# Idle products in float32, and a cast moved from GpSimd to VectorE, in the opening of a Fourier-filter and ELU-network kernel

## The chip, the core and the metric

The kernel runs on one core of a Trainium2 chip. A core has five engines that work at the same time, each through its own queue of instructions in order: TensorE (matrix products; PE in the profile, with PEld for its weight loads), VectorE (DVE), ScalarE (ACT), GpSimd (POOL) and SyncE (SP, which issues most transfers). They share an on-chip memory (SBUF) and the accumulation banks that TensorE writes (PSUM). Sixteen DMA engines move data; GpSimd's transfers appear in the profile as queue q0, SP's as q1, and instruction fetches as q8 and q14.

The metric is the device time of one execution in microseconds (us), lower is better. Three runs of the kernel before took 878.45, 878.87 and 879.24 us; their median is 878.87.

## What is computed

Eight sequences of 3008 positions and 256 channels go through a Fourier filter and then, as 24064 tokens, through a two-layer network with ELU between the layers:

```python
X = np.fft.rfft(x, axis=1)                  # x: (8, 3008, 256)
Yr = Xr @ w_r - Xi @ w_i + b_r              # complex product with a 256 x 256 weight
Yi = Xr @ w_i + Xi @ w_r + b_i
Yr, Yi = soft_threshold(Yr, 0.01), soft_threshold(Yi, 0.01)
y = np.fft.irfft(Yr + 1j * Yi, n=3008, axis=1)
h = y.reshape(24064, 256) @ w_in            # 256 x 2048
g = np.where(h > 0, h, np.exp(np.minimum(h, 0)) - 1)
out = g @ w_out                             # 2048 x 256
```

## The kernel before

**Tiling.** 3008 is 47 x 64, and each transform is two stages of small matrix products with a re-arrangement through DMA between them. For every sequence ("batch" below) there are the units

- A: the first stage of the forward transform, six units. `unit_A` multiplies a part of x (tiles `xt0` to `xt2`) by the matrix `M1` and copies the PSUM result to a tile `A`; in the opening a transfer (`place`, L194, on SP's queue) then puts it into the tile `Z`, which holds the arrangement that the next stage needs;
- X: the second stage, eight units. `unit_X` multiplies `Z` by `M2` into the tile `XT` (8 products of 96 columns a unit, L234);
- M: the product with the complex weight, from `wcat_r` = [w_r | w_i] and `wcat_s` = [-w_i | w_r], with bias and soft threshold, giving tiles `Y`;
- B and Y: the two stages of the inverse transform (`Bz`, stored to the DRAM tile `DB`, loaded again as `Bs`, and then `yT`, the tokens).

The network runs over 376 steps (`front`, `elu`, `back`), each of which takes 512 tokens and two of the 16 blocks of hidden units. TensorE multiplies by w_in (L1071), ScalarE takes the exponential (L1083), GpSimd and VectorE finish ELU (L1122, L1112), TensorE multiplies by w_out (L1143). The transform of the next batch is spread over the steps of the present one.

**The opening.** Batch 0 has nothing to hide behind, so its transform stands alone ahead of the first step. Its order is written out by hand (`manual_schedule`): each engine executes the instructions in the order in which the source issues them.

1. Constants. GpSimd makes index rows, issues the six loads of batch 0's x, and later waits for w_r and w_i (`w_r_f`, `w_i_f`, two loads on SP's queue). VectorE computes the angles of M1, M2 and M3; ScalarE takes the sines.
2. The six A units (`fA`). ScalarE copies each result, SP issues the placement into Z: nine transfers for the six units. Behind these on SP's queue stand the loads of w_r and w_i, three small ones of the bias, and the first quarter of w_in (`load_w_in(0)`).
3. The eight X units. Their PSUM banks are three tiles of two banks (`pre2`), and unit 7 takes two single banks (`apart`). X0, X2, X4, X6 and half of X7 are copied by ScalarE; X1, X3, X5 and the other half of X7 by VectorE.
4. The M units and the inverse of batch 0, with VectorE's scaling of w_in's quarters (`scale_w_in`, L919) put between.

**Idle products.** TensorE's granted clock depends on how busy it has been, and the kernel multiplies a tile of ones (`busy`, 128 x 512 in bfloat16) by itself into a PSUM bank that nobody reads. `idle_pe(n)` issues n such products (L601): 12 ahead of the A units, 0, 0, 1, 2, 2, 0 after the six A units (in `fA`, L831), 21 between the A and the X units (L890), and one after each of X0, X1 and X2 (L940). The 21 use a second bank, which a copy of the last A unit has to release.

**GpSimd between w_i and batch 1.** Four casts to bfloat16 make wcat_r and wcat_s (L871 to L874); the last, L874, is the negated one. Then come the identity `idm` (L875), three loads of batch 1's x of 1 MB each (`load_x`, L118) and half of w_out, also 1 MB (`load_w_out`, L914), all on queue q0.

**After the X units.** VectorE takes the absolute value of M3's angles (L952), the bias copy (L961), two multiplications for M3 (L962, L965), then threshold steps (L346, L399), bias additions (L292) and the scalings of w_in. `load_w_in(1)` is issued in the M stage, behind a store of DB on SP's queue.

The lines in question, as they stand:

```python
        pool.tensor_copy(wcat_r[:, :, D : 2 * D], w_i_f[:])
        pool.tensor_scalar(wcat_s[:, :, 0:D], w_i_f[:], -1.0, None, ALU.mult)
        pool.tensor_scalar(idm[:], prow, pcol[:], None, ALU.is_equal)
    ...
    load_w_in(0)
    for ci in range(3):
        load_x(1, ci)
    load_w_out(0)
    for u in range(8):
        unit_X(0, u, alone=True, on_dve=u in (1, 3, 5), apart=u == 7)
        if u < 3:
            idle_pe(1)
```

Of the kernel before, what the change touches and what calls it, by code (L numbers as in the profile page):

```python
# [8 lines left out]
ALU = mybir.AluOpType  # L9
AF = mybir.ActivationFunctionType  # L10
BF16 = mybir.dt.bfloat16
F32 = mybir.dt.float32
# [17 lines left out]
def kernel(  # L30
# [11 lines left out]
    nc = tc.nc  # L42
    P = nc.NUM_PARTITIONS

    B, S, D = x.shape
# [17 lines left out]
    wcat_s = constp.tile([P, 2, 2 * D], BF16, name="wcat_s")  # L63
# [157 lines left out]
    def unit_X(b, u, alone=False, on_dve=False, apart=False):  # L221
        g, dt = (u % 4, u // 4) if b > 1 else (u // 2, u % 2)
        if u == 0:
            XT_of[b] = xtp.tile([P, 2, 2, K1 * N2], BF16, name="XT", tag="XT")
        XT = XT_of[b]
        if apart:
            psv = [t[:].rearrange("p (k j) -> p k j", j=P) for t in two_banks(pre1, "mps1")]
        else:
            ps = unit_ps("xps", alone)
            psv = [ps[:].rearrange("p a (k j) -> p (a k) j", j=P)]  # L230
        nk = 8 // len(psv)
        for kk in range(8):
            k = 8 * g + kk
            nc.tensor.matmul(  # L234
                psv[kk // nk][:, kk % nk, 0 : 4 * K1],
                lhsT=Z[:, k, dt * P : dt * P + P],
                rhs=M2[:, k].rearrange("p c m -> p (c m)"), start=True, stop=True,
            )
        for h, v in enumerate(psv):
            k0 = 8 * g + nk * h  # L240
            evac(
                XT[:, dt].rearrange("p c (m s) -> p c m s", s=NS)[:, :, :, k0 : k0 + nk],
                v[:, :, 0 : 4 * K1].rearrange("p k (c m) -> p c m k", c=2),
                bool(h) if apart else on_dve,
            )
# [348 lines left out]
    busy = constp.tile([P, 512], BF16, name="busy")  # L594
    nc.vector.memset(busy[:], 1.0)
    ips = [pre1.tile([P, 512], F32, name="ips", tag="mps1")]

    def idle_pe(n):

        for _ in range(n):  # L600
            nc.tensor.matmul(ips[-1][:], lhsT=busy[:, 0:P], rhs=busy[:], start=True, stop=True)  # L601

    bias_p = wk4.tile([P, 2 * D], BF16, name="bias_p", tag="Bs")
    nc.vector.memset(bias_p[:], 0.0)
    idle_pe(12)
    xts = []
    for ci in range(3):
        xt = constp.tile([P, 8, D], F32R, name=f"xt{ci}")
        xts.append(xt)
    with tc.tile_pool(name="stagep", bufs=1) as stagep:  # L610
# [24 lines left out]
        w_r_f, w_i_f = (wk3.tile([P, 2, D], F32, name="yb", tag="yb") for _ in range(2))  # L635
# [7 lines left out]
        dve, pool = nc.vector, nc.gpsimd  # L643
# [161 lines left out]
        def sines(g, c):  # L805
            nc.scalar.activation(
                M2[:, 16 * g : 16 * g + 16, c, :],
                (v2, a2)[c][g][:].rearrange("p s k t -> p s (k t)"), AF.Sin,
                bias=0.0, scale=TURN * (1.0 + c),
            )  # L810
# [17 lines left out]

        def fA(u):
            unit_A(0, u, alone=True, apart=u == 5)  # L830
            idle_pe((0, 0, 1, 2, 2, 0)[u])  # L831

        points(0)
        wraps(0)
# [12 lines left out]
        for u in range(3):  # L847
            fA(u)
        fA(3)
        fA(4)  # L850
        fA(5)
        for k in range(3):
# [18 lines left out]
        pool.tensor_copy(wcat_r[:, :, 0:D], w_r_f[:])  # L871
        pool.tensor_copy(wcat_s[:, :, D : 2 * D], w_r_f[:])
        pool.tensor_copy(wcat_r[:, :, D : 2 * D], w_i_f[:])
        pool.tensor_scalar(wcat_s[:, :, 0:D], w_i_f[:], -1.0, None, ALU.mult)  # L874
        pool.tensor_scalar(idm[:], prow, pcol[:], None, ALU.is_equal)  # L875
        for k in range(3):
            nc.sync.dma_start(bias_p[32 * k : 32 * k + 1, :], bps[:, k])
# [9 lines left out]
        dve.tensor_scalar(w3[:], v3[:], CMAGIC, -CMAGIC, ALU.add, ALU.add)  # L887
        dve.tensor_tensor(w3[:], v3[:], w3[:], ALU.subtract)  # L888
        sines(1, 1)
        idle_pe(21)  # L890

    gatep = ctx.enter_context(tc.tile_pool(name="gatep", bufs=2))
    late2 = ctx.enter_context(tc.tile_pool(name="late2", bufs=2))
# [42 lines left out]
    load_w_out(0)  # L936
    for u in range(8):
        unit_X(0, u, alone=True, on_dve=u in (1, 3, 5), apart=u == 7)
        if u < 3:
            idle_pe(1)  # L940
    zeroth.close()
    pre2, pre1 = (
        first.enter_context(
# [402 lines left out]
```

## Time and profile before

| | us |
|---|---|
| runs: median (lowest to highest) | 878.87 (878.45 to 879.24) |
| the profiled execution: its time | 877.70 |
| the profiled execution: its span | 875.9 |
| TensorE busy in the span | 864.6 |
| ScalarE busy | 712.5 |
| VectorE busy | 667.7 |
| GpSimd busy | 584.6 |

The profile is a record of one execution: for each instruction its engine, start and length, and for each transfer when its packets moved. The span goes from the first to the last instruction; the profiled execution's own time, 877.70, lies 1.8 above its span and 1.17 below the median of the runs. Rows of a timeline read "start, length, engine, source line, operation, result<-operands, shapes, count", where a bracket gives the idle time ahead of the instruction and what ended it. The starts and lengths of matrix products overlap, because they are pipelined. Rows of a stretch read "from:to, length, busy time of each engine (instructions), granted TensorE clock as a share of full speed, busy share of the DMA engines, GB/s". The lines that carry the argument stand in the prediction.

### The profile page before, as it was taken

The page shows a single profiled execution, that of the slowest core. Times are in us where ns is not written, and L with a number is a line of the kernel's source. Part 1 is how long each engine was busy: PE and PEld are TensorE (multiplying, and loading weights), DVE is VectorE, ACT ScalarE, POOL GpSimd, SP SyncE. Part 2 cuts the span into 40 slices and gives each one's busy share as a digit, 9 for nine tenths or more (in the row PEclk, how much of TensorE's full clock was granted, in tenths as well). Part 3 has the DMA queues.
Part 4 walks back from the last instruction along what each step waited for, and adds up shares of the span by engine and source line. Part 5 has one row for each costly group of instructions (what it writes and reads, how often), then busy time and mean ns, then how long its engine had stood idle before and what let it go on. Part 6 is the DMA issues. An engine that isn't in the chain of part 4 may idle for free.

```text
span 875.9 us, 18565 instructions
## 1 busy us (share of the span) xinstructions
PE 864.6 (99%) x6779; PEld 676.4 (77%) x6779; DVE 667.7 (76%) x1118; ACT 712.5 (81%) x1247; POOL 584.6 (67%) x852
## 2 busy tenths in 40 slices
PE   8999999999999999999999999999999999999997
PEld 5568677877788877887778877787877887787776
DVE  8698778687776877768867788677777777788775
ACT  6678788888978889798887988879888798876664
POOL 6662550798757886588856888459874697734664
PEclk9999999999999999999999999999999999999999
DMA  7898337643384324743365432653337313250111
GB/s 239 278 256 242 104 93 200 183 134 85 101 241 141 97 74 124 238 126 104 93 178 163 158 105 77 191 163 126 100 82 223 93 34 91 73 145 25 35 40 49
DMA packets 115852, 116.11 MB, mean 133 GB/s; under 512 B 11552, under 2 KB 106528, under 8 KB 112400
## 3 DMA queue, kind: packets, MB, share of 16 engines
q1 hardware_dynamic: 109504, 87.40, 35.3%
q0 software_dynamic: 5968, 27.26, 9.7%
q8 instruction: 53, 0.87, 0.4%
q14 instruction: 39, 0.32, 0.1%
q10 hardware_dynamic: 288, 0.26, 0.1%
HBM read 53.28 MB, written 48.23 MB: 116 GB/s over the span
## 4 chain that ended last, share of the span: by engine, by line
PE 91%; DVE 4%; POOL 3%; issue 1%; DMA 0%; ACT 0%; SPq 0%; DVEq 0%; POOLq 0%
PE ps_o L1143 39%; PE hps L1071 34%; PE mps L324 5%; PE xps L234 3%; PE mps L1071 2%; PE yps L586 2%; PE bps L425 2%; PE aps L188 2%; PE mps L282 2%; POOL Y L340 1%; POOL yb L336 0%; POOL clip L339 0%; DVE gT L1112 0%; PE pre L282 0%; POOL Y L369 0%
## 5 line engine op out<-in xcount | busy, mean ns | idle before, releaser
L1112 DVE SCALAR_TENSOR_TENSOR gT<-Et,hps 128x512 fp32r<-128x512 f32 x630 | 403.0, 683 | 136.4 <-POOL Et L1122 126.6
L1143 PE MATMUL ps_o<-w_out_r,gT 128*128 128x256 f32 x3008 | 477.4, 302 | 0.0
L1143 PEld LDWEIGHTS ps_o<-w_out_r,gT 128*128 128x128 f32 x3008 | 404.3, 189 | 48.1 <-DVE osb L1155 0.2
L1122 POOL TENSOR_SCALAR Et<-Et 128x512 f32<-128x512 f32 x482 | 287.3, 615 | 209.2 <-ACT Et L1083 207.7
L1071 PE MATMUL hps<-yT,w_in_s 128*128 128x512 bf16 (+7 forms) x1620 | 366.2, 353 | 0.2
L1083 ACT ACTIVATE Et<-hps 128x512 f32<-128x512 f32 x514 | 282.5, 610 | 41.2 <-PE hps L1071 37.4
L1071 PEld LDWEIGHTS <-w_in_s 128*128 128x128 bf16 x1728 | 144.0, 98 | 104.0 <-issue 12.0
L1081 ACT ACTIVATE Et<-hps 128x512 f32<-128x512 f32 x192 | 104.5, 597 | 42.1 <-PE hps L1071 41.7
L1086 ACT ACTIVATE Et<-Et 128x512 f32<-128x512 f32 x192 | 110.5, 632 | 0.0
L340 POOL TENSOR_TENSOR Y<-yb,clip 128x512 bf16<-128x512 f32 x72 | 92.7, 1288 | 6.0
L336 POOL TENSOR_TENSOR yb<-yb,bias_bc 128x256 f32<-128x256 f32 x72 | 53.2, 739 | 11.3 <-DVE yb L331 11.2
L147 ACT CAST XT<-xps 128x768 bf16<-128x768 f32 x58 | 46.6, 804 | 17.0 <-PE xps L234 17.0
L331 DVE TENSOR_TENSOR yb<-mps,yb 128x512 f32<-128x512 f32 x72 | 49.8, 692 | 7.2
L147 ACT CAST yT<-yps 128x752 bf16<-128x752 f32 x56 | 44.1, 787 | 13.7 <-PE yps L586 13.5
L1114 DVE SCALAR_TENSOR_TENSOR gT<-hps,Et 128x512 fp32r<-128x512 f32 x78 | 50.2, 686 | 3.6 <-PE hps L1071 0.5
L147 ACT CAST A<-aps 128x1024 bf16<-128x1024 f32 x41 | 41.7, 1019 | 10.7 <-PE aps L188 4.9
L339 POOL TENSOR_SCALAR clip<-yb 128x512 f32<-128x512 f32 x72 | 44.1, 613 | 6.3
L147 ACT CAST Bz<-bps 128x1024 bf16<-128x1024 f32 x41 | 41.6, 1014 | 5.3 <-PE bps L425 5.0
L330 DVE TENSOR_TENSOR yb<-mps,bias_bc 128x256 f32<-128x256 f32 x72 | 30.5, 423 | 17.5 <-PE mps L324 15.7
L324 PE MATMUL mps<-wcat_s,XT 128*128 128x256 bf16 x288 | 43.3, 273 | 0.0
L1155 DVE COPY osb<-ps_o 128x512 f32<-128x512 f32 x46 | 31.7, 690 | 5.4 <-PE ps_o L1143 3.4
L234 PE MATMUL xps<-M,Z 128*128 128x96 bf16 x504 | 33.1, 211 | 2.8 <-DVE A L888 2.2
(203 smaller groups left out, 671.2 us busy)
## 6 DMA issues: line engine op xcount, KB each, us to landing
xt<-in_x_dram POOLq DMA_DIRECT2D x21, 1024.0 KB, 5.4
out_dram<-osb SPq DMA_DIRECT2D x158, 128.0 KB
Bs<-DB SPq DMA_DIRECT2D x30, 384.0 KB
Yx<-Y SPq DMA_DIRECT2D x168, 64.0 KB
DA<-A SPq DMA_DIRECT2D x19, 512.0 KB
DB<-Bz SPq DMA_DIRECT2D x19, 512.0 KB
Z<-DA SPq DMA_DIRECT2D x21, 384.0 KB
xt<-in_x_dram POOLq DMA_DIRECT2D x6, 512.0 KB, 6.4
```

The source lines that it names most:

```text
L147: nc.scalar.copy(dst, src)
L234: nc.tensor.matmul(psv[kk // nk][:, kk % nk, 0 : 4 * K1], lhsT=Z[:, k, dt * P : dt * P + P], rhs=M2[:, k].rearrange("p c m -> p (c m)"), s ...
L324: nc.tensor.matmul(out_, lhsT=lhs[:, dt] if lhs is not None else sum_of(dt, ch)[:, oc : oc + P], rhs=w[:, dt, :], start=(dt == 0), stop=(d ...
L336: nc.gpsimd.tensor_tensor(yb[:, D : 2 * D], yb[:, D : 2 * D], bias_bc[:, D : 2 * D], ALU.add)
L340: nc.gpsimd.tensor_tensor(Y_of[b, q][:, i, :], yb[:], clip[:], ALU.subtract)
L1071: nc.tensor.matmul(hps[s][:, c0:c1], lhsT=w_in_s[:, dt, ft * P : ft * P + P], rhs=yT_of[b][:, dt, t0 : t0 + c1 - c0], start=(dt == 0), sto ...
L1081: nc.scalar.activation(Et[:, s], hps[s], AF.Relu, scale=-1.0)
L1083: nc.scalar.activation(Et[:, s], hps[s], AF.Exp)
L1086: nc.scalar.activation(Et[:, s], Et[:, s], AF.Exp, scale=-1.0)
L1112: nc.vector.scalar_tensor_tensor(o, e, -1.0, h, ALU.add, ALU.max)
L1122: nc.gpsimd.tensor_scalar(e, e, 1.0, 0.0, ALU.min, ALU.max)
L1143: nc.tensor.matmul(po[q][:, i_ % 2, :], lhsT=gT[:, s, i_ * P : i_ * P + P], rhs=w_out_r[:, ft, :], start=(ft == 0 and i_ % 2 == 0), stop=( ...
```

## The change

Three edits, all in the opening. An idle product now reads the same tile as float32, 128 x 256, with its 256 columns taken twice, and there are 3 and 6 of them where there were 12 and 21. Those between the A units and between the X units go. The negated cast of w_i goes from GpSimd, where it stood ahead of the identity, to VectorE, between its copies of X5 and X7.

```diff
     def idle_pe(n):
 
+        ones = busy[:].bitcast(F32)
         for _ in range(n):
-            nc.tensor.matmul(ips[-1][:], lhsT=busy[:, 0:P], rhs=busy[:], start=True, stop=True)
+            nc.tensor.matmul(
+                ips[-1][:].rearrange("p (a b) -> p a b", a=2), lhsT=ones[:, 0:P],
+                rhs=ones.unsqueeze(1).to_broadcast([P, 2, 256]), start=True, stop=True,
+            )
...
-    idle_pe(12)
+    idle_pe(3)
...
         def fA(u):
             unit_A(0, u, alone=True, apart=u == 5)
-            idle_pe((0, 0, 1, 2, 2, 0)[u])
...
-        pool.tensor_scalar(wcat_s[:, :, 0:D], w_i_f[:], -1.0, None, ALU.mult)
...
-        idle_pe(21)
+        idle_pe(6)
...
     for u in range(8):
         unit_X(0, u, alone=True, on_dve=u in (1, 3, 5), apart=u == 7)
-        if u < 3:
-            idle_pe(1)
+        if u == 5:
+            nc.vector.tensor_scalar(wcat_s[:, :, 0:D], w_i_f[:], -1.0, None, ALU.mult)
```

Source lines of the changed kernel lie 2 to 4 higher from here on: the idle products are L602, the cast L942.

## The prediction

> **What bounds the kernel now.** I read the page first, then stretches of the span, then the order of time in the first 50 us. On the page TensorE is busy 99% of the span.
>
> ```profile
> PE 864.6 (99%) x6779; PEld 676.4 (77%) x6779; DVE 667.7 (76%) x1118; ACT 712.5 (81%) x1247; POOL 584.6 (67%) x852
> ```
>
> The stretches (length, then busy us of PE, PEld, DVE, ACT, POOL, granted clock, DMA share, GB/s) show where that average hides something:
>
> ```profile
> 30.00:57.00 27.00, 25.75 (x219) 13.64 (x218) 21.82 (x40) 21.45 (x44) 14.06 (x19) 1.00 1.03 309
> 57.00:873.00 816.00, 813.26 (x6381) 645.01 (x6379) 621.75 (x1003) 671.99 (x1182) 550.37 (x780) 1.00 0.43 124
> ```
>
> From 57 us on TensorE idles 2.7 us in 816, so whatever is gained or lost before that is carried to the end one for one; no edit touches anything later. The opening is latency. Its chain of waits reads (start, length, what):
>
> ```profile
> 22.34 0.61 issue
> 22.95 0.62 PE xps L234 x8
> 23.57 0.43 PE ips L601
> 24.00 0.64 PE xps L234 x8
> ...
> 28.34 0.81 ACT XT L147
> ```
>
> Two places decide. The first is X0, the X unit that starts at 22.95. The second is VectorE, which stands still until 43.60 for a transfer (timeline of VectorE; brackets: idle before, and what ended it):
>
> ```profile
> 43.60 0.43 DVE L919 TENSOR_SCALAR w_in_s<-w_in_f 128x512 bf16<-128x512 f32 x1 [1.48 <-DMA w_in_f<-in_moe_w_in_dram]
> 43.94 0.68 DVE L346 SCALAR_TENSOR_TENSOR Y<-mps,clip 128x512 bf16<-128x512 f32 x1
> ...
> 45.34 0.74 DVE L399 SCALAR_TENSOR_TENSOR Y<-mps,gT 128x256 bf16<-128x256 f32 x2
> ```
>
> Behind that one wait stand two L346, a copy and both L399, which end at 46.08, and the inverse transforms need those. Why is this second quarter of w_in late? It travels on SP's queue (q1), issued behind a store of DB. Two DMA views, of 36 to 39 us and of 39 to 43 us (MB, share of 16 engines):
>
> ```profile
> q0 software_dynamic: 881, 1.08, 143.4%
> ```
>
> ```profile
> q1 hardware_dynamic: 1640, 1.21, 92.5%
> ```
>
> From 36 to 39 only GpSimd's queue (q0) moves data; SP's follows when that is drained. So w_in lands when it does because of when GpSimd issued batch 1's x and half of w_out:
>
> ```profile
> 25.03 1.51 POOL L874 TENSOR_SCALAR wcat_s<-yb 128x512 bf16<-128x512 f32 x1
> 26.52 0.62 POOL L875 TENSOR_SCALAR idm<-prow,pcol 128x128 bf16<-128x128 f32 x1
> 27.09 1.86 POOL L118 DMA_DIRECT2D xt<-in_x_dram  x3
> ```
>
> ```profile
> 25.50:26.00 0.50, 0.13 (x1) 0.50 0.00 0
> ```
>
> The last row (length, DVE busy, clock, DMA share, GB/s) says that the DMA engines stood empty just before.
>
> **The change part by part.**
>
> *The cast leaves GpSimd.* L874's 1.51 us go. The identity, three x loads and w_out behind it move up by that, x to 25.6, into an empty stretch of DMA. q0 drains 1.5 us sooner, and so do, on q1, the DB stores, w_in's second quarter and the Bs load that waits for the last DB store: w_in lands at 42.1. VectorE then needs the 2.48 us that it needs now (43.60 to 46.08): L399 ends at 44.6. Gain on this path 1.5.
>
> *The cast joins VectorE,* between X5's copy and X7's. Its nearest relative is the scaling of w_in:
>
> ```profile
> L919 DVE TENSOR_SCALAR w_in_s<-w_in_f x6: 419/557/809, 38.1 to 55.8; 128x512 bf16<-128x512 f32 x6
> ```
>
> I take the median, 0.56 us; 0.42 and 0.81 are the ends. Nothing hides it, since X7's products are ready by then; X7's half copy, L952 and M's second product, which needs this weight, queue behind it. The idle products removed from X pay for it:
>
> *No products between X units.* The chain shows 0.43 us for each of three, among X units of 0.64, all at half clock:
>
> ```profile
> 23.00:23.20 0.20, 0.20 (x6) 0.95 0.83 276
> ...
> 26.60:26.80 0.20, 0.20 (x9) 1.00 0.00 0
> ```
>
> ```profile
> L145 DVE CAST XT<-xps 128x768 bf16<-128x768 f32 x3 | 2.8, 955 | 3.5 <-PE xps L234 3.5
> ```
>
> ```profile
> 28.68 0.56 DVE L145 CAST XT<-mps 128x384 bf16<-128x384 f32 x1
> 29.15 1.08 DVE L952 TENSOR_SCALAR A<-A 128x768 int32<-128x768 int32 x1
> ```
>
> Without them X1 ends at 22.95 + 0.62 + 0.64 = 24.2, X3 at 25.5 and X5 near 26.8. VectorE's copies of 0.96 then run 24.2 to 25.2, 25.5 to 26.5 and 26.8 to 27.75, the cast to 28.3, X7's half to 28.9, against 29.24 now: 0.35 earlier, 0.1 to 0.5 by the cast's ends. Banks do not hold TensorE up (X4 needs X1's, free at 25.2, and comes at 25.5). ScalarE, at 0.81 a copy, ends X6 near 27.95 instead of 29.15, so M starts 1.2 earlier on TensorE, 0.35 on VectorE. The last input of L399 comes from ScalarE:
>
> ```profile
> 43.47 1.02 ACT L390 ACTIVATE gT<-mps,lam_n 128x256 f32<-128x256 f32 x2 [0.15 <-PE mps L384]
> ```
>
> Its end, 44.49, moves to about 44.1, and with half of L399's 0.74 the end is 44.5: the transfer's 44.6 still decides. With no gain here it is 44.86, the whole gain 1.2; with a loss of 0.4 it is 0.8.
>
> *No products between A units.* Five at 0.22 us (4.71 / 21 below) would move the last A copy up by about 0.9. I credit nothing, because placing Z sets X0:
>
> ```profile
> 16.03 4.71 PE L601 MATMUL ips<-busy 128*128 128x512 bf16 x21
> ...
> 17.45 1.00 SPq L869 DMA_DIRECT2D yb<-in_w_r_dram  x1
> ...
> 22.95 0.62 PE L234 MATMUL xps<-M,Z 128*128 128x96 bf16 x8 [2.21 <-DVE A L888]
> ...
> 23.34 0.61 POOL L871 CAST wcat_r<-yb 128x512 bf16<-128x512 f32 x1 [7.64 <-DMA yb<-in_w_r_dram]
> ```
>
> ```profile
> 16.00:18.00 2.00, 2.00 (x12) 0.91 (x11) 1.83 (x8) 1.77 (x3) 0.00 (x0) 1.00 0.50 152
> ```
>
> X0's named releaser, L888, was over at 22.34; the load of w_r, next after Z in SP's queue, is issued at 17.45 and lands only at 23.34. At 16 to 18 half of the DMA engines are busy, with Z: a backlog, which earlier copies lengthen. Ends of this term: 0 to 0.9.
>
> *Float32 products.* Each is built as two weight loads and two multiplies with a 4-byte operand; the opening has 46 PE instructions fewer. No row shows one:
>
> ```profile
> 1.45 5.05 PE L601 MATMUL ips<-busy 128*128 128x512 bf16 x12 [1.45 <-DVE busy L595]
> 6.15 4.15 PE L180 MATMUL aps<-xt,M1d 128*128 128x256 f32 x32
> ```
>
> From below, four 256-column float32r products at 4.15 / 32: 0.52 us. From above, (22.95 - 15.1) / 6 = 1.3 us, or the second set delays X0. I take four bf16 products, 0.88 us, near the middle. Then three at half clock fill 1.45 to about 6.5, as twelve do now, and six end at 20.4 instead of 20.7: neutral, and the half clock at 23.2 stays.
>
> The Trainium skill, in "FP8 and Floating Point Precision", TensorE Precision Notes, states four passes through the array for true float32. With bf16 products at 0.22 us that is an estimate of 0.88 us, and this term of the sum is zero by it as well; no run here shows the operation.
>
> **Sum.** Profiled execution 877.70 (span 875.9 and 1.8 around it) - 1.5 = 876.2. That execution lies 1.17 below the median of the runs, 878.87, so the forecast is 878.87 - 1.5 = 877.4. Its own range is a gain of 0.8 to 2.4 (1.5 + 0.9): 876.5 to 878.1.
>
> **The rivals.**
>
> *An instruction fetch leaves Z's way (876.5).* DMA view of 17.0 to 18.2; stretch before it; stretch of TensorE later:
>
> ```profile
> q8 instruction: 1, 0.02, 4.6%
> ```
>
> ```profile
> 0.00:17.20 17.20, 15.75 (x95) 11.62 (x96) 14.99 (x61) 11.79 (x13) 13.70 (x45) 1.00 0.76 242
> ```
>
> ```profile
> 22.00:22.20 0.20, 0.00 (x0) 1.00 0.18 42
> ```
>
> One packet of instructions holds one DMA engine for 0.046 x 16 x 1.2 = 0.9 us, when 95 + 96 PE instructions have started. At 22.0 most engines are idle (0.18) while X0 waits: a straggler. With 46 instructions fewer only about 190 stand before X0, so the fetch may come after Z. Then Z and w_r land 0.9 sooner and GpSimd gains 1.5 + 0.9 = 2.4; X0 starts at 22.0, perhaps without losing the clock, and VectorE, whose own chain ends at 22.34, reaches L952 near 26.5, so the transfer decides: 878.87 - 2.4. Against it: PE's sequencer runs ahead of what has started, so the trigger may lie before X0's wait. "Runtime: NRT & Kernel Launch" of the Trainium skill, Instruction fetch mechanics, states blocks of 256 instructions, whose cost is mostly hidden; by that this rival is worth nothing.
>
> *The gain is swallowed (878.5).* x drains sooner, but another transfer, or VectorE, busy 21.8 of 27 us, binds before 57. For it: DMA share 1.03 there. Against: all that q1 carries behind q0 moves too.
>
> *The products are too long: slower (881).* Place: the six before X0. At 1.7 us each the first three, mostly at half clock, end at 8.9, A starts 2.5 later and ends at 17.6, the six end at 27.8. VectorE then needs 0.7 to X1's end, three copies, the cast and a half: L952 at 32.4, 3.2 late. L399 ends at 44.86 + 3.2 = 48.1 against 46.08: +2. It decides from about 1.45 us each, where X0 comes at 25.7 and L399 ends at 46. For it: no row shows this operation. Against: that is nearly seven bf16 products in one.
>
> **How the numbers follow.** Forecast 0.46, fetch 0.28, swallowed 0.13, slower 0.13. Within 0.2% (1.76 us) no change can be told here; the three runs lie 0.79 apart. Faster: 0.42 of the forecast (where the A units' part comes on top) and 0.95 of the fetch: 0.19 + 0.27 = 0.46. Slower: 0.9 of the slower case and a tenth of the swallowed one: 0.13. Same: 0.41. The range 875.4 to 879.5 goes from the fetch case with the A part to just beyond the swallowed one; it leaves out most of the slower case and a few hundredths below.
>
> **What would show it.** In the changed profile: the identity on GpSimd at 25.0 and x loads from 25.6; VectorE's wait for w_in ended near 42.1, L399's end near 44.6; the second set of products ending at 20.2 to 20.7; half clock from about 23.2 to 26.6; a cast of 0.4 to 0.8. X0 near 22.0 would show the fetch rival right. X0 after 23.5, behind the products, would show the slower one. If w_in lands at 42 and TensorE's steady stretch starts no earlier, the gain is swallowed.

## The result and the profile after

The changed kernel takes 875.54 us (median of 6 runs, 874.85 to 875.97), the kernel before beside it 878.94: 3.4 us less, ratio 0.9961 with a 95% interval of 0.9948 to 0.9974. The profiled execution took 874.85 (span 873.1). The forecast was 877.4 in a range of 875.4 to 879.5: the time lies at the lower end of the range, and the gain is 3.4 us where 1.5 was forecast. Executions of this kernel differ among themselves by the stretches of halved clock that fall into the opening; these will turn out to be about a third of the gain.

GpSimd and VectorE in the changed kernel (timeline, the columns as in the prediction):

```profile
21.84 0.92 POOL L874 CAST wcat_r<-yb 128x512 bf16<-128x512 f32 x1 [6.18 <-DMA yb<-in_w_r_dram]
...
23.87 0.61 POOL L877 TENSOR_SCALAR idm<-prow,pcol 128x128 bf16<-128x128 f32 x1
24.45 1.97 POOL L118 DMA_DIRECT2D xt<-in_x_dram  x3
```

```profile
25.27 0.42 DVE L942 TENSOR_SCALAR wcat_s<-yb 128x512 bf16<-128x512 f32 x1
...
40.13 0.43 DVE L921 TENSOR_SCALAR w_in_s<-w_in_f 128x512 bf16<-128x512 f32 x1 [1.27 <-DMA w_in_f<-in_moe_w_in_dram]
...
41.87 0.75 DVE L399 SCALAR_TENSOR_TENSOR Y<-mps,gT 128x256 bf16<-128x256 f32 x2
```

Batch 1's x is issued at 24.45 instead of 27.09: 1.5 of that is the cast, the rest comes from w_r, for which GpSimd's first cast waits (it ends 1.2 earlier). VectorE's wait for w_in's second quarter ends at 40.13 instead of 43.60, and L399 ends at 42.62 instead of 46.08. From 36 to 39 us, where before only q0 moved data, SP's queue now moves data too (DMA view of these 3 us):

```profile
q1 hardware_dynamic: 813, 0.78, 75.6%
q0 software_dynamic: 320, 0.31, 52.1%
```

TensorE:

```profile
1.44 4.99 PE L602 MATMUL ips<-busy 128*128 128x512 f32 x6 [1.44 <-DVE busy L595]
...
14.43 2.19 PE L180 MATMUL mps<-xt,M1d 128*128 128x256 f32 x16 [0.75 <-DMA xt<-in_x_dram]
16.45 5.32 PE L602 MATMUL ips<-busy 128*128 128x512 f32 x12
21.61 1.18 PE L234 MATMUL xps<-M,Z 128*128 128x96 bf16 x24
...
45.55 0.83 PE L559 MATMUL one<-M,Bs 96*128 96x94 bf16 x16 [0.83 <-DMA Bs<-DB]
46.85 1.04 PE L1073 MATMUL hps<-yT,w_in_s 128*128 128x512 bf16 x3
```

Twelve multiplies are six products, so a product takes 5.32 / 6 = 0.89 us. X0 starts at 21.61 instead of 22.95, without a wait, straight behind the second set. The L559 bracket is new: TensorE now waits 0.83 us for the Bs load. The last row (L1073) is the first product with w_in, which starts the steady part; before, it stood at 49.73:

```profile
49.73 1.04 PE L1071 MATMUL hps<-yT,w_in_s 128*128 128x512 bf16 x4
```

From this product to the end of the span are 875.9 - 49.73 = 826.2 us before and 873.1 - 46.85 = 826.3 after. So the whole difference between these two executions lies ahead of it. In the profiled executions below the rest of the span is 826.1 to 826.5 as well, in all but one (827.8, w_in early in the kernel before, where the halved clock lasts beyond this start), so they can be read by this start.

### The profile page after: what moved, and what is told of

Read it like the earlier page. It is cut to its first block, busy times and chain, and to the rows that moved or that the text cites. A ratio compares the mean times of both kernels' runs of the same rounds, so it can differ in the third digit from the quotient of the medians.

```text
span 873.1 us, 18416 instructions
## 1 busy us (share of the span) xinstructions
PE 857.1 (98%) x6654; PEld 675.4 (77%) x6756; DVE 667.4 (76%) x1119; ACT 712.2 (82%) x1247; POOL 583.0 (67%) x851
## 4 chain that ended last, share of the span: by engine, by line
PE 89%; POOL 4%; DVE 2%; DMA 2%; issue 1%; ACT 1%; SPq 0%; DVEq 0%; POOLq 0%; ACTq 0%
PE ps_o L1145 38%; PE hps L1073 32%; PE mps L324 5%; PE xps L234 2%; PE mps L1073 2%; PE yps L586 2%; PE bps L425 2%; PE aps L188 2%; PE mps L282 2%; POOL Y L340 1%; DMA xt<-in_x_dram 1%; DVE gT L1114 1%; POOL yb L336 1%; PE ips L602 1%; DMA DB<-Bz 1%
## 5 line engine op out<-in xcount | busy, mean ns | idle before, releaser
L1073 PE MATMUL hps<-yT,w_in_s 128*128 128x512 bf16 (+6 forms) x1528 | 360.1, 352 | 5.0 <-DVE gT L1114 0.2
L1073 PEld LDWEIGHTS <-w_in_s 128*128 128x128 bf16 x1728 | 144.1, 98 | 103.9 <-issue 12.4
L252 POOL TENSOR_TENSOR XS<-XT 128x512 bf16<-128x512 bf16 x30 | 34.1, 1158 | 2.4 <-ACT XT L147 1.4
```

What stands on the lines that cost most here:

```text
L1073: nc.tensor.matmul(hps[s][:, c0:c1], lhsT=w_in_s[:, dt, ft * P : ft * P + P], rhs=yT_of[b][:, dt, t0 : t0 + c1 - c0], start=(dt == 0), sto ...
```

## The experiments

Three theories. *Queue* (the forecast): the cast delayed the issue of batch 1's x, and with q0 everything that SP's queue carries behind it. *Fetch* (the rival): fewer TensorE instructions ahead of X0 move an instruction packet out of Z's way. *Clock*, formed after the first four runs: TensorE's wait behind w_in halves its clock in some executions, and the change shortens that wait.

### The parts, one by one

The cast alone, the products alone, bf16 products of the same length, and the number of instructions alone.

Cast only:

```diff
-        pool.tensor_scalar(wcat_s[:, :, 0:D], w_i_f[:], -1.0, None, ALU.mult)
...
             idle_pe(1)
+        if u == 5:
+            nc.vector.tensor_scalar(wcat_s[:, :, 0:D], w_i_f[:], -1.0, None, ALU.mult)
```

> The kernel before with the cast alone moved from GpSimd to VectorE; all idle products as before. Forecast's path (GpSimd issues batch 1's x earlier by the 1.51 us of the cast): x issued at 25.6, w_in's second quarter lands near 42.1, gain 1.2 to 1.5 (877.4 to 877.7). Rival, the whole gain comes from the fetch and the clock: gain under 0.5 (above 878.4). X0 stays at 22.9 and the clock is halved from 23.2 under both.

Measured: 875.92 (ratio 0.9970 with its 95% interval of 0.9960 to 0.9980). Most of the gain, 2.6 us by the ratio and 3.1 by the medians, more than the 1.2 to 1.5 expected. X0 came at 22.57, w_r at 22.80 instead of 23.34, and no stretch of the profiled execution's opening was halved, although neither X0 nor the clock at 23.2 was expected to change; so 0.5 of the earlier issue of x is w_r's and not the cast's, and why w_r came earlier is open.

```profile
25.10 2.00 POOL L118 DMA_DIRECT2D xt<-in_x_dram  x3
```

```profile
41.46 0.43 DVE L918 TENSOR_SCALAR w_in_s<-w_in_f 128x512 bf16<-128x512 f32 x1 [1.29 <-DMA w_in_f<-in_moe_w_in_dram]
```

Products only (the changed kernel, the cast back on GpSimd):

```diff
+        pool.tensor_scalar(wcat_s[:, :, 0:D], w_i_f[:], -1.0, None, ALU.mult)
         pool.tensor_scalar(idm[:], prow, pcol[:], None, ALU.is_equal)
...
-        if u == 5:
-            nc.vector.tensor_scalar(wcat_s[:, :, 0:D], w_i_f[:], -1.0, None, ALU.mult)
```

> The changed kernel with the cast left on GpSimd ahead of the identity. Fetch theory: the packet moves after Z, X0 at 21.3 to 21.7, full clock throughout, GpSimd's first cast near 21.8 and batch 1's x near 25.9 (24.45 + 1.5), so a gain of 1.0 to 1.5 without the cast (877.4 to 877.9). Rival, the cast gives nearly everything: gain under 0.5 (above 878.4). If the two parts add up, this gain and that of the cast alone make 3.4 together; if one chain binds after the first 1.5 us, they make more than 3.4.

Measured: 878.93 (1.0003, 0.9994 to 1.0011). No gain, although X0 came at 21.98 and x was issued at 26.18, both within 0.3 us of the fetch theory, which had expected a gain of 1.0 to 1.5 and the full clock throughout. Its profile (VectorE, TensorE, then stretches of 3.41 us) shows where the earlier X went:

```profile
43.09 0.43 DVE L922 TENSOR_SCALAR w_in_s<-w_in_f 128x512 bf16<-128x512 f32 x1 [3.85 <-DMA w_in_f<-in_moe_w_in_dram]
```

```profile
41.02 0.29 PE L518 MATMUL lateB<-M,Y 64*128 64x32 bf16 x8
44.17 0.29 PE L518 MATMUL lateB<-M,Y 64*128 64x32 bf16 x8 [2.85 <-DVE Y L346]
```

```profile
41.06:44.47 3.41, 0.55 (x17) 0.33 (x17) 1.39 (x4) 0.47 (x2) 0.14 (x1) 1.00 0.61 187
44.47:47.88 3.41, 2.92 (x36) 2.21 (x36) 2.29 (x7) 1.35 (x5) 1.10 (x2) 0.50 0.62 162
```

M is done earlier, w_in comes hardly earlier (43.09), so VectorE waits 3.85 us for it and TensorE 2.85 for VectorE. TensorE is busy 0.55 of 3.41 us there, and in the next stretches it is granted half of its clock (0.50): the clock records of this execution give 44.47 to 51.30. The front that was won became a longer wait, and the wait, it seems, cost clock; the run with this gap filled, below, tests that.

The changed kernel with bf16 products of the same total length:

```diff
-    idle_pe(3)
+    idle_pe(12)
...
-        idle_pe(6)
+        idle_pe(24)
```

with the product itself as in the kernel before.

> The changed kernel, but its 3 and 6 float32 idle products are 12 and 24 bf16 ones again, of the same total length (about 0.22 us each at full clock). The cast stays on VectorE and there is none between A or X units. 36 more TensorE instructions stand ahead of X0 than in the changed kernel, 4 fewer than before. Fetch theory (the number of TensorE instructions ahead of X0 decides when the first instruction packet is fetched): the packet moves near 17 us again, X0 comes at 22.5 to 23, the granted clock is halved from about 23.2, batch 1's x is issued near 25.6, and 1 to 1.5 us of the gain are left (877.4 to 878). Rival, the time of the products or the places between units decides: X0 near 21.6, no halved clock, the whole gain (875.5).

Measured: 876.26 (0.9972, 0.9961 to 0.9984); X0 at 21.65, x issued at 24.46, the packet at 22 us. The fetch theory's numbers failed: 36 more instructions did not bring the packet back to 17. The profiled execution has a stretch of half clock at 43.6, after one in which TensorE was busy 1.97:

```profile
40.17:43.58 3.41, 1.97 (x45) 1.34 (x44) 2.53 (x7) 1.47 (x5) 1.28 (x4) 1.00 0.24 57
43.58:47.00 3.42, 3.42 (x40) 2.42 (x34) 2.36 (x5) 1.99 (x5) 0.52 (x1) 0.50 0.89 225
```

The changed kernel with 46 instructions more:

```diff
+    for _ in range(23):
+        nc.tensor.matmul(ips[-1][:, 0:8], lhsT=busy[:, 0:P], rhs=busy[:, 0:8], start=True, stop=True)
     idle_pe(3)
```

> The changed kernel with 23 more products of 8 columns ahead of the first set of float32 products: 46 more TensorE instructions ahead of X0, as many as the change took away, for 1 to 2 us of TensorE's time that lies ahead of x's arrival. Fetch theory: the packet moves near 17 us, w_r lands near 23.3, X0 at 22.5 to 23, batch 1's x near 25.6, total 877 to 878. Rival (length or kind of the products): X0 near 21.6, no packet before Z has landed, total 875.3 to 876.

Measured: 876.05 (0.9970, 0.9960 to 0.9980), the profiled execution 875.18; X0 at 21.87, x issued at 24.48. The packet moved at 14.7 us, ahead of Z's last part and not at 17 as in the kernel before, and X0 and x came about as in the changed kernel (21.61 and 24.45):

```profile
q8 instruction: 1, 0.02, 6.4%
```

(DMA view of 14 to 15 us.) So the fetch theory falls as the main source of the time: the number of instructions can be put back at a cost that this comparison does not show, and with the cast on GpSimd an earlier X0 is worth nothing. That a packet at 17 us costs nothing is not shown, because neither run put it back there. The cast is worth 2.6 to 3.1 us, nearly twice its own length. That excess was open.

### Is it the queue, and what is the excess?

The kernel before with the cast left on GpSimd, but behind the DMA issues:

```diff
-        pool.tensor_scalar(wcat_s[:, :, 0:D], w_i_f[:], -1.0, None, ALU.mult)
...
     load_w_out(0)
+    nc.gpsimd.tensor_scalar(wcat_s[:, :, 0:D], w_i_f[:], -1.0, None, ALU.mult)
```

> The kernel before with all its idle products; the negated cast stays on GpSimd, but behind batch 1's x loads and w_out. Queue theory (the cast delayed the issue of batch 1's x, and with it everything that SP's queue carries behind it): x is issued at 25.1 to 25.6 as when the cast is on VectorE, w_in's second quarter lands at 41 to 42, and the time is that of the cast-only kernel, 875.9 (875.4 to 876.6). Rival, GpSimd has too much work or VectorE's copy of the cast is what pays: no gain, 878.5 to 879.3. Point of doubt: M's second product needs the cast, which ends near 30.1; M starts at 30.05 in the profile before, so a wait of up to 0.5 us may come back.

Measured: 876.24 (0.9973, 0.9964 to 0.9983), as with the cast on VectorE. GpSimd has the same work; only the order on its queue differs:

```profile
24.86 1.85 POOL L118 DMA_DIRECT2D xt<-in_x_dram  x3
26.53 1.08 POOL L913 DMA_DIRECT2D w_out_r<-in_moe_w_out_dram  x1
27.47 1.88 POOL L936 TENSOR_SCALAR wcat_s<-yb 128x512 bf16<-128x512 f32 x1
```

The queue theory is shown, and moving the work to VectorE has no part in the gain that this comparison can tell.

The kernel before, profiled a second time:

> The kernel before, unchanged, to see a second profiled execution of it. Clock theory: a typical execution, near 879, shows at least one 3.4-us stretch of halved clock more than the first profile of it (877.70, one stretch at 23.2), behind TensorE's wait for w_in's second quarter (43 to 51 us). Rival: the same single stretch at 23.2, and the difference between 877.70 and 879 lies elsewhere. Median 878.9 to 879.1 either way.

Measured: 878.60 (1.0000, 0.9991 to 1.0009). The execution that was profiled is the longest of its ten, 880.19 (span 878.4). VectorE, then stretches:

```profile
43.64 0.43 DVE L919 TENSOR_SCALAR w_in_s<-w_in_f 128x512 bf16<-128x512 f32 x1 [3.12 <-DMA w_in_f<-in_moe_w_in_dram]
...
45.38 0.74 DVE L399 SCALAR_TENSOR_TENSOR Y<-mps,gT 128x256 bf16<-128x256 f32 x2
```

```profile
20.99:24.41 3.42, 1.75 (x28) 1.22 (x27) 1.60 (x3) 1.52 (x2) 1.09 (x2) 1.00 0.69 202
41.50:44.92 3.42, 1.30 (x24) 0.90 (x23) 1.28 (x4) 1.16 (x4) 0.97 (x3) 1.00 0.62 195
44.92:48.33 3.41, 2.91 (x42) 2.10 (x35) 2.29 (x7) 1.34 (x5) 1.09 (x2) 0.50 0.57 135
48.33:51.74 3.41, 3.41 (x36) 2.59 (x35) 2.42 (x4) 1.90 (x4) 0.00 (x0) 0.50 1.00 271
```

This is the key pair. In the first profile of the same kernel the clock was halved at 23.2, in this one it is not; there X and M were slower, here VectorE waits 3.12 us for w_in instead of 1.48, and L399 ends at the same time, 46.12 and 46.08. The halved clock at 23.2 cost nothing, because w_in came last anyway. Here the clock is halved from 44.9 to 51.7 instead, behind the wait, and the first product with w_in starts at 52.08 instead of 49.73: 2.35 us later for two stretches.

The products-only kernel with ten idle products in its gap:

```diff
-    turn_B(1, ps=two_banks(lateB, "lateB"))
+    pb = two_banks(lateB, "lateB")
+    for _ in range(10):
+        nc.tensor.matmul(pb[0][:], lhsT=busy[:, 0:P], rhs=busy[:], start=True, stop=True)
+    turn_B(1, ps=pb)
```

> The kernel with the products changed and the cast left on GpSimd, and 10 more bf16 idle products (2.2 us) put where its TensorE stood still for 2.85 us, between the last M product and the second half of the first turned B unit. Clock theory (the earlier X units only lengthened TensorE's wait behind w_in, and the granted clock was halved for 6.8 us after it): no halved clock between 41 and 52, median 876.9 to 877.6, so 1.3 to 2.0 better than without them. Rival (the clock there costs nothing, the transfer alone decides): 878.6 to 879.2 as without them.

Measured: 877.37 (0.9988, 0.9979 to 0.9997): 1.6 better than without them by the medians and 1.3 by the ratios, within the range expected. The profiled execution is the longest of its eleven (878.71) and contradicts the detail: the products fill 40.3 to 42.6, but a gap of 1.63 us is left, and a stretch with 1.32 busy is followed by half a clock once.

```profile
40.32 2.32 PE L1010 MATMUL lateB<-busy 128*128 128x512 bf16 x10
42.57 0.29 PE L518 MATMUL lateB<-M,Y 64*128 64x32 bf16 x8
44.50 0.29 PE L518 MATMUL lateB<-M,Y 64*128 64x32 bf16 x8 [1.63 <-DVE Y L346]
```

```profile
42.96:46.38 3.42, 1.32 (x35) 1.05 (x36) 2.70 (x7) 0.65 (x3) 0.75 (x2) 1.00 0.20 41
46.38:49.79 3.41, 3.41 (x36) 2.46 (x31) 2.33 (x6) 1.86 (x4) 0.34 (x1) 0.50 0.90 243
```

Their effect is seen in the number of executions. One stretch lowers the mean granted clock of an execution by 3.41 / 2 / 876 = 0.0019, so a mean of 0.999 or above leaves no room for one in the opening. A lower mean need not come from the opening: in every profiled execution the clock is halved for the last 0.3 to 2.8 us of the span too, which takes up to 0.0016, and one listed with 0.998 (w_in early and x late) has no halved stretch in the opening. So the counts are lower bounds. Of the executions timed, so many have 0.999 or above:

| kernel | at 0.999 or above | their median |
|---|---|---|
| before (all runs with a clock listed) | 5 of 77 | 877.41 |
| products only | 0 of 11 | - |
| products only, gap filled | 8 of 11 | 877.34 |
| cast only | 5 of 8 | 875.77 |
| cast behind the loads | 10 of 11 | 876.22 |
| bf16, same length | 4 of 7 | 875.19 |
| 46 instructions more | 6 of 8 | 875.66 |
| changed kernel (both times) | 9 of 11 | 875.11 |

In the kernel before, the time goes with the mean: the 16 executions listed with 0.995 have a median of 879.4, the 25 with 0.997 one of 878.1, and the 5 of the table 877.4. The gap-filled kernel, freed of the halved clock, is as long as the kernel before freed of it: the products themselves bring nothing while the cast stands ahead of x. With the cast moved they go with 0.7 us more (875.77 to 875.11, in ranges that overlap). Whether that is the products, their number or the packet, these runs do not separate.

### What binds next

The last of batch 1's three x loads behind the second half of w_out, in the changed kernel:

```diff
-    for ci in range(3):
+    for ci in range(2):
         load_x(1, ci)
...
     load_w_out(1)
+    load_x(1, 2)
```

> The changed kernel with the last of the three x loads of batch 1 (1 MB) moved behind the second half of w_out on GpSimd's queue. Queue theory: 1 MB less ahead of SP's transfers, w_in's second quarter lands by 38.5 (40.1 in the changed kernel), VectorE's wait for it (1.27 us) goes, the Bs load starts 0.5 to 1.3 earlier, total 874.2 to 875.0. Rival, what is pushed back collides with Bs, the later quarters of w_in and batch 1's A units: 875.5 to 877.

Measured: 874.34 (0.9950, 0.9937 to 0.9963). VectorE's wait for w_in is gone; both scalings run in one piece, straight behind L346:

```profile
39.11 1.95 DVE L921 TENSOR_SCALAR w_in_s<-w_in_f 128x512 bf16<-128x512 f32 x2
```

The load of w_in's second quarter right behind the first, in the kernel before, in the changed one, and there with x late as well:

```diff
     load_w_in(0)
+    load_w_in(1)
...
     fB(3)
-    load_w_in(1)
```

> The kernel before with the load of w_in's second quarter issued right behind the first quarter's, ahead of batch 1's x; cast on GpSimd, idle products as before. Queue theory (VectorE's and TensorE's wait for this quarter behind q0 is what the cast's place costs, with the halved clock that follows it): w_in lands before 28, no wait for it near 40 to 44, no halved clock between 43 and 52, and the Bs load behind the DB stores binds instead (stores landing near 43.5 to 45); 876.0 to 877.5, so 1.2 to 2.7 better than before with the cast unmoved. Rival (what pays is GpSimd's time or the cast's place itself): 878.3 to 879.2.

Measured: 876.98, ratio 0.9992 (0.9977 to 1.0008). Six of the twelve executions took 875.1 to 876.7, as the queue theory says, and the other six 877.2 to 881.3; the first six are those with a mean clock of 0.999 or above. So with the cast still on GpSimd, w_in alone brings the gain in half of the executions. The profiled one (881.28) shows a wait that nobody had expected (GpSimd, SP, TensorE; then the DMA view of 44 to 49 us and a stretch of 3.41 us):

```profile
42.66 0.96 POOL L914 DMA_DIRECT2D w_out_r<-in_moe_w_out_dram  x1
```

```profile
43.61 0.33 SPq L456 DMA_DIRECT2D Bs<-DB  x1
```

```profile
49.41 0.86 PE L559 MATMUL one<-M,Bs 96*128 96x94 bf16 x9 [4.53 <-DMA Bs<-DB]
```

```profile
q0 software_dynamic: 975, 1.00, 97.4%
q1 hardware_dynamic: 102, 0.27, 24.2%
```

```profile
44.39:47.80 3.41, 0.49 (x8) 0.11 (x4) 1.01 (x2) 0.82 (x2) 0.00 (x0) 1.00 1.21 251
```

GpSimd holds the second half of w_out back by a gate, a copy of one column that waits for L399. L399, done earlier, opened it at 42.66, ahead of the Bs load, which still waited for the DB stores until 43.61. So 1 MB on q0 went first, the 192 KB of Bs came 5.8 us after their issue, and the clock was halved behind that wait, from 47.80 to 54.63. That the other long executions have the same wait is likely and not shown: one of them has a profile.

> The changed kernel with the load of w_in's second quarter issued right behind the first quarter's. The wait of 1.27 us for it goes, the DB stores have 512 KB less between them and land near 41 (42.22 in the changed kernel): 874.2 to 875.0. Rival, the Bs load was the last to come in any case and x starts later behind 512 KB more: 875.4 to 876.

Measured: 874.17 (0.9950, 0.9938 to 0.9962), at the lower edge of what was expected. Here the Bs load was issued at 42.17, ahead of w_out's 42.68, and came in time.

> Both transfer changes on the changed kernel: w_in's second quarter early and the last x load of batch 1 late. If transfers still bind with x late alone (874.34), another 0.3 to 0.8: 873.5 to 874.1. If the engines bind there already, the same as with x late alone: 874.2 to 874.6.

Measured: 874.88 (0.9960, 0.9948 to 0.9972): neither of the two expectations. Its profiled execution (874.12) has the earliest first product of all, 46.09, but its six executions lie between 873.81 and 876.49. Why they scatter is open; the clock is not it, since the one at 876.49 has a mean of 0.999.

> The changed kernel once more, for a second profiled execution of it and a comparison with the versions above on one chip. Expected 875.4 to 875.8; X0 between 21.4 and 22.4 by where the instruction packet falls; no halved clock, or one stretch of 3.4 us near 43 to 47.

Measured: 874.89 (0.9962, 0.9950 to 0.9974), a little below the 875.4 to 875.8 expected; X0 at 22.34, x issued at 24.97, no halved clock in the opening. On the same chip and beside the same runs of before, the version with w_in early is 0.7 us shorter and the one with x late was 874.34 on another chip; the intervals overlap with the changed kernel's, so neither is shown to beat it.

### All profiled executions together

Starts and ends are those of the rows named; "halved" are the granted clock's stretches of 3.41 us between L399 and 55 us.

| kernel | X0 | x issued | L399 ends | halved | first w_in product | from L399's end | time |
|---|---|---|---|---|---|---|---|
| before | 22.95 | 27.09 | 46.08 | 0 | 49.73 | 3.65 | 877.70 |
| before, again | 22.98 | 27.07 | 46.12 | 2 | 52.08 | 5.96 | 880.19 |
| products only | 21.98 | 26.18 | 45.57 | 2 | 51.58 | 6.01 | 879.88 |
| products only, gap filled | 21.37 | 26.30 | 45.89 | 1 | 50.73 | 4.84 | 878.71 |
| before, w_in early | 21.77 | 26.01 | 42.79 | 2 | 51.72 | 8.93 | 881.28 |
| cast only | 22.57 | 25.10 | 43.94 | 0 | 47.59 | 3.65 | 875.77 |
| cast behind loads | 22.22 | 24.86 | 44.59 | 0 | 48.24 | 3.65 | 876.20 |
| bf16, same length | 21.65 | 24.46 | 43.26 | 1 | 48.10 | 4.84 | 876.26 |
| 46 instructions more | 21.87 | 24.48 | 43.30 | 0 | 46.95 | 3.65 | 875.18 |
| changed | 21.61 | 24.45 | 42.62 | 0 | 46.85 | 4.23 | 874.85 |
| changed, again | 22.34 | 24.97 | 43.06 | 0 | 46.96 | 3.90 | 874.88 |
| changed, x late | 22.40 | 25.01 | 43.12 | 0 | 46.77 | 3.65 | 874.78 |
| changed, w_in early | 22.09 | 24.75 | 42.81 | 0 | 46.46 | 3.65 | 874.65 |
| changed, both | 21.72 | 24.44 | 42.44 | 0 | 46.09 | 3.65 | 874.12 |

What follows L399 takes 3.65 us at full clock, 4.84 with one halved stretch and 6.0 with two, so 1.2 us each; in the kernel before with w_in early the wait for Bs comes on top. In the first execution of the changed kernel the Bs load adds 0.6 instead and takes back part of what L399 won; in the second 0.25 is left, behind a row that names VectorE's copy.

The queue shows in one more number. In the ten executions with both loads in their old place, VectorE's scaling of w_in's second quarter starts 15.3 to 17.1 us after the issue of x, whether M was done early or late.

## Why the prediction was right, and where it was short

- **The cast leaves GpSimd, gain 1.5: right.** With the cast alone moved L399 ends at 43.94; the forecast was 44.6, and 0.5 of the difference is the earlier w_r. Without halved stretches the cast alone brings 877.41 - 875.77 = 1.6 us, and behind the loads on the same engine 1.2. The "swallowed" rival was half seen: something else did bind afterwards, the Bs load, with 0.6 us in one of the two profiled executions.
- **The sum against one profiled execution: the step that failed, for the clock's part of the excess.** The prediction took the 1.17 us between the first profile (877.70) and the median (878.87) for a constant that both kernels have. It was not. It was the halved clock behind the wait for w_in, which that profile by luck did not have, and which the second profile of the same kernel shows with 6.8 us. The change shortens this wait (TensorE's bracket behind L346 is 0.27 us in the changed kernel, 2.12 in the second profile of before) and the stretches went with it: 9 of 11 executions without one instead of 5 of 77. By the table, of the 3.4 us some 2.3 are earlier transfers and work (877.41 to 875.11 among executions without a stretch), the other 1.1 clock. This split is rough: it rests on five executions of the kernel before, and a harmless stretch like that at 23.2 is counted as one that costs. Of the 2.3 the cast alone gives 1.6, about the forecast; the other 0.7 the sum had put at nothing, although the prediction allowed up to 0.9 for it at an end of its range and in the fetch rival.
- **"The half clock at 23.2 stays": wrong, and of no account.** It stood in one of the two profiles of before and cost nothing there. The prediction priced X and M by it, so it had M 0.35 earlier on VectorE, where L954 moved from 29.15 to 26.07.
- **The fetch rival: the sign came true, the price did not.** The packet moved from 17 to 22 us and X0 to 21.61 (forecast of that rival: 22.0), and its time, 876.5, lay nearer than the forecast's. But with the cast on GpSimd an X0 at 21.98 brought nothing (878.93), and 46 instructions put back cost no more than the comparison can tell (876.05). Apart from that kernel, X0 lay at 21.77 to 22.98 in the five profiled executions where the packet moved at 15 to 17 us, and at 21.37 to 22.40 in the eight where it moved later than 20: two groups that overlap but lie 0.6 apart in the mean. So a part of the 0.7 may be the packet's; it is not shown.
- **Products between A units, 0: right, for another reason.** Not Z's placing but x held the A units back: TensorE waited 0.75 us for it at 14.43.
- **The float32 product, 0.88: measured 0.89.** The place of the second set was wrong: it ends at 21.77 and not at 20.2 to 20.7, because x came late and the A units with it, so that in this execution the products and not Z set X0. The kernel with bf16 products of the same length has X0 at the same place (21.65). In the second profile of the changed kernel the set starts at 15.94, and X0 waits 1.09 us behind it. **The cast on VectorE, 0.56: measured 0.42,** its lower end.

## What to carry to other kernels

A busy share of 67% says nothing about an instruction that stands ahead of a DMA issue: look what waits behind it on that engine's queue, and behind those transfers on the others. When the profiled execution is clearly shorter than the median, the difference is a question and not an offset: profile a second execution, and look for a wait after which the granted clock falls. When a load is moved forward, ask which gate it opens early, and what large transfer then gets ahead of a small one that everybody waits for.

## What was not expected of the hardware

- The granted clock is halved in stretches of 3.41 us whose phase differs between executions (the first clock record lies between 4.5 and 7.4 us). Up to 55 us, stretches at full clock with TensorE busy for 0.49, 0.55, 1.20, 1.30 and 1.32 us were followed by a halved one; those with 1.70, 1.75, 1.80, 1.85, 1.91, 1.93 and more than 2.1 were not. Only one does not fit: 1.97, followed by a halved one. Where two halved ones follow each other, TensorE was busy 1.8 to 2.9 us of the first. "TensorE: Matmul & The Clock Gate" of the Trainium skill, What's actually happening, names an idle window of about 3.4 us as the condition; the length agrees, but here a window need not be idle: 1.32 of 3.41 us busy was little enough.
- A transfer of 192 KB on SP's queue came 5.8 us after its issue while 1 MB ran on q0: in those 5 us q0 moved 1.00 MB and q1 0.27. "DMA: Bandwidth & Descriptors" of the Trainium skill, Queues, rings and completion order, has each engine alternate between the queues packet by packet; an equal share of the bytes does not follow from that, and the trace does not show one.
